# All eight transposes of a visit ahead of the two copies that empty them

## The chip, the cores and the metric

One core of a Trainium2 chip runs the whole program. The metric is the device time of one execution in microseconds; the kernel before takes 685.97 us, the median of 3 runs (685.84 to 686.15). The engines are TensorE (PE, with its weight loads shown apart as PEld), VectorE (DVE), ScalarE (ACT), GpSimd (POOL) and SyncE (SP, which here only issues DMA transfers). Every engine works through its own queue in the order in which the instructions stand there, and waits on semaphores that the others raise.

## The reference

A recurrent retention block (4 batches, 8 heads, 768 steps, head size 64) is followed by a two-layer block with a SiLU between the layers:

```python
gamma = 1.0 - 2.0 ** (-5.0 - np.arange(H, dtype=np.float32))
for t in range(S):
    state = gamma[None, :, None, None] * state + np.einsum('bhd,bhe->bhde', k[:, :, t], v[:, :, t])
    y[:, :, t] = scale * np.einsum('bhd,bhde->bhe', q[:, :, t], state)
x = y.transpose(0, 2, 1, 3).reshape(B * S, H * D)      # 3072 x 512
h = x @ w_in                                           # 512 x 2048
g = h * (1.0 / (1.0 + np.exp(-h)))
out = g @ w_out                                        # 2048 x 512
```

The two weight matrices arrive as 64-bit floats, read as pairs of 32-bit words.

## The kernel before

The 768 steps are cut into 6 chunks of 128, and a chunk of one batch is a *unit*: 24 units, chunk by chunk. A function `visit()` is called 26 times; call m works on three units at once. `stage_t(m)` transposes unit m: four 128x128 transposes of its keys (`kf`) and four of its queries (`qf`) on PE into one tile `tp` that spans two PSUM banks, keys in the first bank and queries in the second; two ACT copies bring them to SBUF as `kt` and `qt` (L289). `stage_y(m - 2)` computes that unit's output and state product on PE into a tile `y` (L305): 24 matmuls in general, fewer in the first chunk, and 16 without the state product in the last. `finish_y` splits `y` into three parts for the products that follow (ACT L364, DVE L365 and L366) and updates the state (ACT L356, DVE L358). `stage_a(m - 1)` computes the scores of unit m - 1 into a tile `sc` (PE L336), and DVE weighs them (`am`, L340). The tiles `tp`, `y` and `sc` share one PSUM pool of two buffers of two banks each, and are asked for in this order. So `sc` of a visit takes the buffer of `tp` of the same visit, and can start only after both copies have emptied it; and the next `tp` takes the buffer of `y`.

Between the visits stand the first-layer products. `product_in(c, f)` makes 12 matmuls (L413, L414, L415) into `ha` and `hb`, two buffers each, which ACT (L417, then the SiLU L419) and DVE (L418, between the two) drain; SP writes the result `g` to DRAM. Chunks 0 and 1 take 32 products, in four groups of eight written out by hand (`phases`): the first half of the weight blocks for chunk 0, then for chunk 1, then the second half for each; from chunk 2 on a visit follows every fourth product. Through the first part of the kernel, the weights are converted from 64 bits and split (`take_w`): per block of 128 rows or columns an ACT operation L172, six DVE operations from L174 to L186, and, for the first layer, two on ACT (L105, L109) and two more on DVE (L107, L110). They are waited for late: the conversions run up to eight blocks ahead of the product that needs them. After the last product the second layer runs (L533 to L535), PE alone setting its pace.

PE's order is that of the code (it is scheduled by hand). The order of ACT, DVE, POOL and SP is chosen by a list scheduler when the program is built, by its own estimate of when each instruction becomes ready; a change in the code on PE therefore moves instructions on the other engines too.

In what follows, visit m is the m-th call, counted from 0. Visits 0 to 5 stand ahead of the first product, visits 6 to 13 between the products of chunks 0 and 1, visits 14 to 23 between those of chunks 2 to 4, and visits 24 and 25 have no transposes left.

Of the kernel before, what the change touches and what calls it, by code (L numbers as in the profile page):

```python
# [12 lines left out]
FP32 = mybir.dt.float32  # L13
# [18 lines left out]
def kernel(  # L32
# [26 lines left out]
    nc = tc.nc  # L59
    B, H, S, D = q.shape  # L60
    DM, DF = moe_w_in.shape
    C = 128
    NC = S // C
    HP = H // 2
# [12 lines left out]
    def pool(name, bufs, **kw):  # L77
        return ctx.enter_context(tc.tile_pool(name=name, bufs=bufs, **kw))
# [6 lines left out]
    one = pool("one", 1)  # L85
# [30 lines left out]
    kqv = {"k": {}, "q": {}, "v": {}}  # L116
# [72 lines left out]
    evac, w_sb = [], {}  # L189
# [23 lines left out]
    ident = const.tile([128, 128], FP32, tag="ident", name="ident")  # L213
# [49 lines left out]
    xt, kt, qt, am, live = {}, {}, {}, {}, {}  # L263

    def banks(name):
        return ps_u.tile([128, 2, 512], FP32, tag="u", name=name)
# [12 lines left out]

    def stage_t(n):  # L280

        tp = banks(f"tp_{n}")
        for i, (name, src, to, bufs) in enumerate((("k", kqv["k"][n], kt, 2),
                                                   ("q", kqv["q"].pop(n), qt, 3))):
            part = tp[:, i].rearrange("p (a t) -> p a t", a=HP)
            for a in range(HP):
                nc.tensor.transpose(part[:, a, :], src[:, 2 * a : 2 * a + 2, :], ident)  # L287
            t = one.tile([128, HP, C], FP32, tag=f"{name}t", name=f"{name}t_{n}", bufs=bufs)
            evac[:] = [nc.scalar.copy(out=t, in_=part).ins]  # L289
            to[n] = t  # L290

    def stage_y(n):

# [88 lines left out]
    def visit():  # L382
        m = visits[0]
        visits[0] += 1
        if m - 2 >= len(units):
            return
        if m < len(units):
            stage_t(m)
        rest = None
        if m >= 2:  # L390
            stage_y(m - 2)
            rest = finish_y(m - 2)
        if 1 <= m <= len(units):
            stage_a(m - 1)
            scale_q(m - 1)
            scale_k(m - 1)
        if rest is not None:
            rest()
        load("k", m + 2)
        load("q", m + 2)  # L400
        load("v", m)
# [114 lines left out]
    for c in range(NC):  # L516
# [8 lines left out]
        for f in range(NF):  # L525
            n = c * NF + f
            split(n + S_AHEAD)
            t = ready.pop(n)
# [7 lines left out]
        for b in range(B):  # L536
            oa, ob = acc[b]
            o = one.tile([128, DM], FP32, tag=("kt", "qt")[b % 2], name=f"o_{c}_{b}",
                         bufs=(2, 3)[b % 2])
# [33 lines left out]
```

## Time and profile before

| | us |
|---|---|
| median of 3 runs | 685.97 |
| the profiled execution | 685.41 |
| its span, first to last instruction | 683.5 |
| PE busy in the span | 639.4 |
| DVE busy | 427.9 |
| ACT busy | 284.4 |

The profile comes from one execution. The span lies inside that execution's time, with 1.9 us around it. A row of a timeline gives the start, the duration, the engine, line and operation, the tiles as output<-input, and how many alike follow each other; in brackets stands the time that the engine idled before the row, and what ended it. A row of the waits names who waited for whom, with the total, the number of waits and the longest. A row of the windows gives the busy time of each engine in one stretch of the span and the TensorE clock that was granted there (1.00 is full). Matmuls overlap in the array, so a group's duration is from its first start to its last end.

### The profile page before, as it was taken

Reading aid. Unit: us, or ns where it says so; the run is one execution under the profiler, and the core shown is the slowest. Engines: PE = TensorE matmul, PEld = TensorE weight load, DVE = VectorE, ACT = ScalarE, POOL = GpSimd, SP = SyncE. Lnnn points to the kernel's source line nnn. Section 1 sums busy time; section 2 is a strip of 40 time slices with the busy share of each in tenths; the row PEclk is TensorE's granted clock in tenths of the full one; section 3 lists DMA queues with packets and bytes.
Section 4 is the critical chain, followed back from the end, with each engine's and each line's share of the span. In section 5 each row is a group of like instructions: output and inputs, shape, how many; then the busy total and the mean of one; then the engine's idle time right before and its main releaser. Section 6 shows DMA issues by size and latency. Waiting matters only on the chain.

```text
span 683.5 us, 11097 instructions
## 1 busy us (share of the span) xinstructions
PE 639.4 (94%) x4288; PEld 520.8 (76%) x4288; DVE 427.9 (63%) x696; ACT 284.4 (42%) x510; POOL 10.6 (2%) x44
## 2 busy tenths in 40 slices
PE   4768889899999999999999999999999999999996
PEld 3656667687877777777788888888888888888885
DVE  5878999995567675756443876546455463734641
ACT  5536545654544444544435795222222221321311
POOL 3000000000000000000000000000000000000000
PEclk9979999999999999999999999999999999999999
DMA  8865766776455666766412775334253352523401
GB/s 201 184 146 147 177 178 203 205 226 217 154 159 165 203 184 200 203 183 193 140 69 83 227 214 156 111 108 151 67 180 91 94 169 78 166 82 123 142 14 62
DMA packets 123061, 103.50 MB, mean 151 GB/s; under 512 B 80000, under 2 KB 88192, under 8 KB 123008
## 3 DMA queue, kind: packets, MB, share of 16 engines
q1 hardware_dynamic: 119552, 96.49, 48.9%
q10 hardware_dynamic: 3456, 6.29, 2.5%
q8 instruction: 34, 0.56, 0.3%
q14 instruction: 19, 0.16, 0.1%
HBM read 66.06 MB, written 36.70 MB: 150 GB/s over the span
## 4 chain that ended last, share of the span: by engine, by line
PE 79%; DVE 9%; ACT 5%; DMA 3%; issue 2%; SPq 1%; ACTq 0%; DVEq 0%
PE ha L413 11%; PE ha L414 11%; PE hb L415 11%; PE ob L535 6%; PE o L533 6%; PE o L535 6%; PE o L534 6%; PE oa L533 6%; PE oa L534 6%; PE y L305 5%; PE sc L336 2%; PE tp L287 2%; DMA wf<-in_moe_w_in_dram 2%; ACT kt L289 1%; DVE g L418 1%
## 5 line engine op out<-in xcount | busy, mean ns | idle before, releaser
L415 PE MATMUL hb<-xt,wi 128*128 128x512 f32 x384 | 151.1, 394 | 3.1 <-DVE xt L366 2.5
L413 PE MATMUL ha<-xt,wi 128*128 128x512 f32 x384 | 152.6, 397 | 0.0
L414 PE MATMUL ha<-xt,wi 128*128 128x512 f32 x384 | 150.2, 391 | 0.0
L460 DVE TENSOR_TENSOR gs<-gr,gs 128x512 fp32r<-128x512 f32 x96 | 62.1, 686 | 93.5 <-ACT gs L458 93.5
L458 ACT ACTIVATE gs<-gr 128x512 fp32r<-128x512 f32 x96 | 53.4, 621 | 139.3 <-issue 131.7
L418 DVE TENSOR_TENSOR g<-g,hb 128x512 f32<-128x512 f32 x96 | 65.8, 685 | 69.4 <-ACT g L417 67.4
L419 ACT ACTIVATE g<-g 128x512 f32<-128x512 f32 x96 | 60.7, 632 | 72.7 <-DVE g L418 71.9
L415 PEld LDWEIGHTS hb<-xt,wi 128*128 128x128 f32 x384 | 72.4, 189 | 21.0 <-DVE xt L366 2.9
L413 PEld LDWEIGHTS ha<-xt,wi 128*128 128x128 f32 x384 | 72.5, 189 | 18.0 <-issue 3.5
L414 PEld LDWEIGHTS ha<-xt,wi 128*128 128x128 f32 x384 | 72.6, 189 | 14.6
L417 ACT ACTIVATE g<-ha 128x512 f32<-128x512 f32 x96 | 56.7, 591 | 60.0 <-PE ha L414 44.0
L535 PE MATMUL ob<-wo,gs 128*128 128x512 f32 x192 | 75.3, 392 | 0.0
L533 PE MATMUL o<-wo,gs 128*128 128x512 f32 x192 | 74.8, 389 | 0.0
L533 PE MATMUL oa<-wo,gs 128*128 128x512 f32 x192 | 74.8, 389 | 0.0
L535 PE MATMUL o<-wo,gs 128*128 128x512 f32 x192 | 74.7, 389 | 0.0
L534 PE MATMUL oa<-wo,gs 128*128 128x512 f32 x192 | 74.7, 389 | 0.0
L534 PE MATMUL o<-wo,gs 128*128 128x512 f32 x192 | 74.7, 389 | 0.0
L461 DVE SCALAR_TENSOR_TENSOR gs<-gs 128x512 fp32r<-128x512 f32 x96 | 61.9, 684 | 0.0
L535 PEld LDWEIGHTS ob<-wo,gs 128*128 128x128 f32 x192 | 36.0, 188 | 8.9 <-DVE o L541 1.5
L535 PEld LDWEIGHTS o<-wo,gs 128*128 128x128 f32 x192 | 36.0, 188 | 7.6
L534 PEld LDWEIGHTS oa<-wo,gs 128*128 128x128 f32 x192 | 36.1, 188 | 7.5
L534 PEld LDWEIGHTS o<-wo,gs 128*128 128x128 f32 x192 | 36.0, 188 | 7.5
(67 smaller groups left out, 693.2 us busy)
## 6 DMA issues: line engine op xcount, KB each, us to landing
gd<-g SPq DMA_DIRECT2D x96, 256.0 KB, 2.8
gr<-gd SPq DMA_DIRECT2D x96, 256.0 KB, 2.7
wf<-in_moe_w_out_dram SPq DMA_DIRECT2D x16, 512.0 KB, 4.2
kf<-in_k_dram SPq DMA_DIRECT2D x24, 256.0 KB, 4.2
qf<-in_q_dram SPq DMA_DIRECT2D x24, 256.0 KB, 4.0
vf<-in_v_dram SPq DMA_DIRECT2D x24, 256.0 KB, 4.3
out_dram<-o ACTq DMA_DIRECT2D x24, 256.0 KB, 2.1
wf<-in_moe_w_in_dram SPq DMA_DIRECT2D x16, 256.0 KB, 3.3
```

The costliest lines, as they stand in the source:

```text
L413: nc.tensor.matmul(ha, lhsT=w[0], rhs=x[0], start=first_, stop=False)
L414: nc.tensor.matmul(ha, lhsT=w[1], rhs=x[1], start=False, stop=last)
L415: nc.tensor.matmul(hb, lhsT=w[2], rhs=x[2], start=first_, stop=last)
L417: nc.scalar.activation(out=hs, in_=ha, func=AF.Copy, scale=ONE_E)
L418: nc.vector.tensor_tensor(out=hs, in0=hs, in1=hb, op=ALU.subtract)
L419: nc.scalar.activation(out=hs, in_=hs, func=AF.Silu)
L458: nc.scalar.activation(out=t[:, 0, :], in_=g, func=AF.Copy, scale=HALF)
L460: nc.vector.tensor_tensor(out=t[:, 1, :], in0=g, in1=high, op=ALU.subtract)
L461: nc.vector.scalar_tensor_tensor(out=t[:, 2, :], in0=t[:, 1, :].bitcast(FP32), scalar=-1.0 / EPS, in1=high, op0=ALU.mult, op1=ALU.add)
L533: nc.tensor.matmul(oa, lhsT=gh, rhs=wo[f][:, 0, :], start=first_, stop=False)
L534: nc.tensor.matmul(oa, lhsT=glo, rhs=wo[f][:, 1, :], start=False, stop=last)
L535: nc.tensor.matmul(ob, lhsT=gm, rhs=wo[f][:, 2, :], start=first_, stop=last)
```

## The change

In `stage_t`, the loop that transposed the keys, copied them, transposed the queries and copied those becomes two loops: all eight transposes first, then the two copies. Tiles, buffers and computing instructions stay the same.

```diff
-        tp = banks(f"tp_{n}")
-        for i, (name, src, to, bufs) in enumerate((("k", kqv["k"][n], kt, 2),
-                                                   ("q", kqv["q"].pop(n), qt, 3))):
-            part = tp[:, i].rearrange("p (a t) -> p a t", a=HP)
+        tp = banks(f"tp_{n}").rearrange("p o (a t) -> p o a t", a=HP)
+        for i, src in enumerate((kqv["k"][n], kqv["q"].pop(n))):
             for a in range(HP):
-                nc.tensor.transpose(part[:, a, :], src[:, 2 * a : 2 * a + 2, :], ident)
-            t = one.tile([128, HP, C], FP32, tag=f"{name}t", name=f"{name}t_{n}", bufs=bufs)
-            evac[:] = [nc.scalar.copy(out=t, in_=part).ins]
-            to[n] = t
+                nc.tensor.transpose(tp[:, i, a, :], src[:, 2 * a : 2 * a + 2, :], ident)
+        for i, (name, to, bufs) in enumerate((("kt", kt, 2), ("qt", qt, 3))):
+            to[n] = one.tile([128, HP, C], FP32, tag=name, name=f"{name}_{n}", bufs=bufs)
+            evac[:] = [nc.scalar.copy(out=to[n], in_=tp[:, i]).ins]
```

The lines behind `stage_t` move up by two: L287 becomes L285, both copies L288, L336 becomes L334 and so on.

On PE, at visit 14 (`tp` is the tile of the transposes, `y` and `sc` those of the two products behind them; a wait is named after the engine or DMA queue that raises the semaphore), the rows before are:

```order
L287 MATMUL tp_2185<-ident,kf_1596 128x128 [waits DMAHW3_49,PE_49]
L287 MATMUL tp_2185<-ident,qf_1598 128x128 [waits DMAHW4_49,Activation_49]
L305 MATMUL y_2198<-vf_1600,kf_1246 64x64 [waits DMAHW1_49,PE_49]
L305 MATMUL y_2198<-am_1717,vf_1600 64x128 x8
L305 MATMUL y_2198<-qt_1544,state_242 64x128 x8
L336 MATMUL sc_2227<-qt_1669,kt_1663 64x128 [waits Activation_49]
```

and those of the change:

```order
L285 MATMUL tp_2185<-ident,kf_1596 128x128 [waits DMAHW4_49,PE_49]
L285 MATMUL tp_2185<-ident,qf_1598 128x128 [waits DMAHW7_49]
L303 MATMUL y_2198<-vf_1600,kf_1246 64x64 [waits DMAHW5_49,PE_49]
L303 MATMUL y_2198<-am_1717,vf_1600 64x128 x8
L303 MATMUL y_2198<-qt_1544,state_242 64x128 x8
L334 MATMUL sc_2227<-qt_1669,kt_1667 64x128 [waits PE_49,Activation_49]
```

PE's order is the same; the transposes of the queries no longer wait for ACT, and `sc` still does.

On ACT, at visit 10 (`g` is drained from the products, `ca`, `wi` and `wil` belong to the weight conversion, `ys` takes `y` away), the rows before are:

```order
L172 ACTIVATE ca_1166<-wf_1014 128x512 [waits DMAHW1_49,DMAHW7_49,DMAHW0_49,DVE_49]
L417 ACTIVATE g_5_1158<-ha_5_1144 128x512 [waits DMAHW4_49,PE_49,Activation_49]
L289 COPY kt_1188<-tp_1183 128x512 [waits PE_49]
L105 ACTIVATE wi_1137<-cs_1128 128x512 [waits DVE_49]
L289 COPY qt_1194<-tp_1183 128x512 [waits PE_49]
L419 ACTIVATE g_5_1158<-g_5_1158 128x512 [waits DVE_49]
```

and those of the change:

```order
L415 ACTIVATE g_5_1158<-ha_5_1144 128x512 [waits DMAHW4_49,PE_49,Activation_49]
L172 ACTIVATE ca_1166<-wf_1014 128x512 [waits DMAHW1_49,DMAHW2_49,DMAHW0_49,DVE_49]
L288 COPY kt_1192<-tp_1183 128x512 [waits PE_49]
L288 COPY qt_1194<-tp_1183 128x512
L417 ACTIVATE g_5_1158<-g_5_1158 128x512 [waits DVE_49]
```

The two copies stand side by side, and the second has no wait of its own: the first already waits for all eight transposes. `ca` has moved between the drain of `ha` and the copies. In the visits of the later chunks (visit 14 among them) the SiLU L419 stays between the two copies, as before.

On DVE, ahead of the weighing of the scores at visit 13 (`am`; `cs`, `cp`, `ca`, `wil` and `wi` belong to the weight conversion), the rows before are:

```order
L107 SCALAR_TENSOR_TENSOR wil_1527<-cs_1517,wi_1526 128x512
L110 SCALAR_TENSOR_TENSOR wi_1526<-wi_1526,wil_1527 128x512
L174 TENSOR_SCALAR cs_1642<-wf_1475 128x512
L179 SCALAR_TENSOR_TENSOR cs_1642<-ca_1641,cs_1642 128x512
L358 TENSOR_TENSOR state_245<-state_245,y_1671 128x256
L181 TENSOR_SCALAR cp_1643<-cs_1642 128x512
L176 TENSOR_SCALAR ca_1824<-ca_1824 128x512
L183 SCALAR_TENSOR_TENSOR cp_1643<-wf_1475,cp_1643 128x512
L340 TENSOR_TENSOR am_1717<-sc_1700,decay 128x1024
```

and those of the change:

```order
L181 TENSOR_SCALAR cp_1518<-cs_1517 128x512
L356 TENSOR_TENSOR state_245<-state_245,y_1671 128x256
L183 SCALAR_TENSOR_TENSOR cp_1518<-wf_1367,cp_1518 128x512
L176 TENSOR_SCALAR ca_1641<-ca_1641 128x512
L186 TENSOR_TENSOR cs_1517<-cs_1517,cp_1518 128x512
L338 TENSOR_TENSOR am_1717<-sc_1700,decay 128x1024
L107 SCALAR_TENSOR_TENSOR wil_1527<-cs_1517,wi_1526 128x512
L278 TENSOR_TENSOR qt_1544<-qt_1544,gq 128x512
L110 SCALAR_TENSOR_TENSOR wi_1526<-wi_1526,wil_1527 128x512
```

`am` has moved from place 199 of DVE's queue to place 192: seven operations of the weight conversion that stood ahead of it now stand behind it. From the visit before that on to the products behind it, the drains and weighings stand two to four microseconds of DVE work nearer the front than before (by the durations that DVE's rows have in the trace); by the drain of the twenty-fourth product both orders have done the same work.

## The prediction

> **What bounds the kernel now.** I read the busy times first, then the same by stages.
>
> ```profile
> PE 639.4 (94%) x4288; PEld 520.8 (76%) x4288; DVE 427.9 (63%) x696; ACT 284.4 (42%) x510; POOL 10.6 (2%) x44
> 0.00:47.00 47.00, 28.09 (x338) 21.45 (x338) 33.77 (x53) 23.06 (x54) 5.16 (x40) 0.93 0.88 191
> 47.00:137.00 90.00, 77.37 (x858) 62.24 (x862) 82.24 (x141) 49.28 (x86) 2.71 (x2) 0.94 0.65 175
> 137.00:155.00 18.00, 17.76 (x95) 14.16 (x88) 16.66 (x31) 8.53 (x16) 0.00 (x0) 1.00 0.78 236
> 155.00:193.00 38.00, 38.00 (x168) 31.01 (x169) 19.60 (x32) 19.95 (x35) 0.00 (x0) 1.00 0.51 169
> 193.00:351.00 158.00, 150.86 (x1328) 123.16 (x1327) 101.88 (x165) 72.03 (x122) 2.72 (x2) 1.00 0.60 177
> 351.00:683.00 332.00, 327.28 (x1515) 268.74 (x1513) 173.73 (x277) 111.60 (x200) 0.00 (x0) 1.00 0.38 121
> ```
>
> A stage's row is its length, then PE, PEld, DVE, ACT and POOL busy, the granted clock, the DMA share and GB/s. The 94% is an average over stages with different limits. From 193 to 351 us (visits 14 to 23) PE is idle for 158.00 - 150.86 = 7.1 us and DVE is busy for only 64%: PE sets the time. From 47 to 137 us (visits 6 to 13) DVE is busy for 82.24 of 90 us and PE for 77.37: there DVE is the fuller engine. Up to 47 us neither is full. Behind 351 us no transpose is left, and I expect nothing to change.
>
> Next, who waited for whom: up to 155 us (first three rows), in its part from 47 to 137 us (the fourth), and from 155 to 352 us (the last).
>
> ```profile
> PE tp L287 <- ACT kt L289: 15.7, 14, 2.8
> PE hb L415 <- DVE xt L366: 2.5, 1, 2.5
> PE sc L336 <- ACT qt L289: 2.1, 3, 1.1
> PE tp L287 <- ACT kt L289: 10.3, 8, 2.8
> PE tp L287 <- ACT kt L289: 6.8, 10, 0.7
> ```
>
> In all 24 visits the transposes of the queries wait for the copy of the keys: 22.5 us in sum, 6.8 of it in the ten late visits. That wait the change takes away. The question is how much comes back as a wait of `sc`, which needs both copies, and how much the full DVE of the early stage swallows.
>
> **The late visits (14 to 23): 6.6 us.** Visit 14, in order of time:
>
> ```profile
> 192.86 0.60 PE L287 MATMUL tp<-ident,kf 128*128 128x128 f32 x4
> 192.88 0.60 ACT L417 ACTIVATE g<-ha 128x512 f32<-128x512 f32 x1 [0.73 <-PE ha L414]
> 193.50 0.59 ACT L289 COPY kt<-tp 128x512 f32<-128x512 f32 x1
> 193.51 0.69 DVE L418 TENSOR_TENSOR g<-g,hb 128x512 f32<-128x512 f32 x1 [2.03 <-ACT g L417]
> 194.13 0.66 PE L287 MATMUL tp<-ident,qf 128*128 128x128 f32 x4 [0.68 <-ACT kt L289]
> 194.23 0.63 ACT L419 ACTIVATE g<-g 128x512 f32<-128x512 f32 x1 [0.15 <-DVE g L418]
> 194.72 0.69 PE L305 MATMUL y<-vf,kf 128*64 128x64 f32 x16
> 194.83 0.59 ACT L289 COPY qt<-tp 128x512 f32<-128x512 f32 x1
> 195.24 1.05 PE L305 MATMUL y<-am,vf 128*64 128x128 f32 x16
> 196.70 1.05 PE L336 MATMUL sc<-qt,kt 64*64 64x128 f32 x32
> ```
>
> Four transposes take 0.60 us, of which the last one's own 0.27 overlaps what follows, so they are about 0.11 apart and the fifth can start some 0.45 us behind the first, at 193.31 instead of 194.13. `y` starts 0.59 us behind that (194.72 - 194.13), at 193.90, and PE is ready for `sc` 1.98 us later (196.70 - 194.72), at 195.88: 0.82 us earlier.
>
> ACT is late next. The first copy now waits for all eight transposes, which end at 193.31 + 0.66 = 193.97; with the 0.04 us that lie between the transposes' end and the copy in these rows it runs from 194.01 to 194.60. The SiLU behind it (its input is ready when L418 ends, 194.20) runs to 195.25 and the second copy to 195.86. So `sc` may start at about 195.9, just when PE is there. I take 0.8 us a visit; the bounds are 0.5 (another 0.3 us of handing over on ACT) and 0.9.
>
> Visits 22 and 23 have a shorter `y`. Visit 23:
>
> ```profile
> 336.04 0.60 PE L287 MATMUL tp<-ident,kf 128*128 128x128 f32 x4
> 337.31 0.66 PE L287 MATMUL tp<-ident,qf 128*128 128x128 f32 x4 [0.68 <-ACT kt L289]
> 339.41 1.05 PE L336 MATMUL sc<-qt,kt 64*64 64x128 f32 x32
> ```
>
> Here `sc` stood 339.41 - 336.04 = 3.37 us behind the first transpose. ACT's chain (copy, SiLU, copy) takes 195.9 - 192.86 = 3.04 us as at visit 14, so it ends last, and 0.3 us is gained. The sum is 8 x 0.8 + 2 x 0.3 = 7.0; I take 6.6, nearer to the lower bound since ACT has nothing to spare, with ends at 4.5 and 7.8.
>
> **The first 47 us: 1.8 us.** The first product that needs a whole chunk starts at 47.22 us, behind DVE's last split L366 (the 2.5 us above). DVE comes to that split through this row:
>
> ```profile
> 42.91 0.69 DVE L365 TENSOR_TENSOR xt<-y,xt 128x512 fp32r<-128x512 f32 x1 [1.79 <-ACT xt L364]
> ```
>
> DVE stood idle for 1.79 us, for a `y` that stands behind two of the waits removed. An earlier `y` gains at most this idle time, then DVE's other work is in the way. The bounds are 0 and 5.4 (all waits of the first six visits, 15.7 - 10.3). I take 1.8.
>
> **Visits 6 to 13: 5.7 us.** PE's waits look large here, and the longest is at visit 10:
>
> ```profile
> 87.91 0.60 PE L287 MATMUL tp<-ident,kf 128*128 128x128 f32 x4
> 89.67 0.67 ACT L172 ACTIVATE ca<-wf 128x512 f32<-128x512 f32 x1 [0.43 <-DVE cs L179]
> 90.23 0.58 ACT L417 ACTIVATE g<-ha 128x512 f32<-128x512 f32 x1
> 90.71 0.58 ACT L289 COPY kt<-tp 128x512 f32<-128x512 f32 x1
> 91.35 0.87 PE L287 MATMUL tp<-ident,qf 128*128 128x128 f32 x4 [2.84 <-ACT kt L289]
> 93.06 1.92 PE L305 MATMUL y<-am,vf 128*64 128x128 f32 x16
> ```
>
> ACT came late to the copy because `ca` ahead of it waited for DVE. The change lets PE go through the transposes and `y` meanwhile, so this wait shrinks to what is left at `sc`. Besides, behind the wait of 2.84 us the same 16 matmuls of `y` take 1.92 us, against 1.05 at visit 14 (the row at 195.24): the granted clock is lower there (0.94 in the stage), and an unbroken PE would keep it.
>
> But DVE decides what of this stays. It has 90 - 82.24 = 7.8 us of idle time in the stage, and PE waits for its drains and weighings, whatever PE gained. Two things let PE run ahead of it. First, order: at visit 13 seven conversion operations move behind `am`. Their cost is from these two rows, between which eight operations of DVE start:
>
> ```profile
> 135.41 0.68 DVE L107 SCALAR_TENSOR_TENSOR wil<-cs,wi 128x512 f32<-128x512 f32 x1
> 139.58 1.22 DVE L340 TENSOR_TENSOR am<-sc,decay 128x1024 f32<-128x1024 f32 x1
> ```
>
> (139.58 - 135.41) / 8 = 0.52 us each, so 3.6 us. Second, idle time: DVE idles partly because its inputs from PE come late; I take a quarter of the 7.8 us, 2.1 with rounding up. Together 5.7 us. The bounds are 0 (DVE's idle time stays, and the work put off is in the way later) and 3.6 + 7.8 = 11.4.
>
> Is the work put off paid for later? These rows speak of it:
>
> ```profile
> 154.13 0.68 DVE L418 TENSOR_TENSOR g<-g,hb 128x512 f32<-128x512 f32 x1
> 154.86 0.50 PE L415 MATMUL hb<-xt,wi 128*128 128x512 f32 x1 [0.24 <-DVE g L418]
> 161.42 0.69 DVE L186 TENSOR_TENSOR cw<-cs,cp 128x512 f32<-128x512 f32 x1 [1.12 <-DMA wod<-cw]
> ```
>
> At 154 us PE runs into DVE's backlog, for 0.24 us; at 161 DVE already idles, and the backlog is gone. A product takes 12 matmuls of 38.00 / 168 = 0.226 us (the row from 155 to 193 us, where PE never idles), 2.7 us, and with two buffers PE can be a product ahead of the drains. So most of 5.7 us can stay; more than about 8 (5.7 and most of a product) would meet the drains around 160 us.
>
> One rule of the skill speaks against this part. Perfetto Trace Analysis in the Trainium skill (section Identifying Performance Opportunities) says to judge by the engine with the highest occupancy in each regime, and to optimize that one first. Here that is DVE with 82.24 of 90 us, by the row above; by the rule alone a change that only takes waits from PE would be worth nothing in these visits. It is the first rival below.
>
> **Sum.** 1.8 + 5.7 + 6.6 = 14.1 us. Against the profiled execution, 685.41 - 14.1 = 671.3; the median of the runs is 0.56 us above that execution, so 671.9 us.
>
> **Rivals.**
> *DVE holds the first 155 us.* All early waits turn into waits for DVE, and only the late visits count: 685.97 - 6.6 = 679.4. For it: DVE's 91% from 47 to 137 us. Against it: DVE itself idled for PE and ACT, and the order puts work behind. Chance 0.10.
> *All named waits go.* Early, the 15.7 us of `tp`, the 2.1 of `sc`, and the slower clock behind the long wait of visit 10 (1.92 - 1.05 = 0.9) vanish, with the 6.6 us late: 685.97 - 25.3 = 660.7. Against it speaks DVE's idle time: of 25.3 - 6.6 = 18.7 us, 13.3 (without the 5.4 of the first six visits) is more than DVE can give up between 47 and 137 us. Chance 0.08.
> *The wait only moves.* ACT hands over later than I reckon, and `sc` waits as long as the transposes did: 686.0. In the late visits this takes a second copy that ends 0.8 us later than worked out; the rows give no cause. Chance 0.03.
> *Slower: the copies stand behind a conversion that waits.* At visit 10 `ca` now stands ahead of both copies, and it needs a weight load and DVE. Before, such waits for the load were 3.5 us in two visits:
>
> ```profile
> ACT ca L172 <- DMA wf<-in_moe_w_in_dram: 3.5, 2, 2.6
> wf<-in_moe_w_in_dram SPq DMA_DIRECT2D x16, 256.0 KB, 3.3
> ```
>
> A load takes 3.3 us to land. If its issue slips behind the loads of keys, which now wait for other transposes, each such visit loses up to 3.3 us at `sc`. It decides from 14.1 / 3.3 = 4.3 visits on; with all of the eight, 685.97 - 14.1 + 26.4 = 698.3, with five 688.4. Chance 0.04.
>
> **How the numbers follow.** The forecast, 671.9, has 0.75. Its own ends are the bounds of its terms: all three at their upper ends give 5.4 + 11.4 + 7.8 = 24.6, but the drains around 160 us let no more than about 8 of the middle term through, and the first is held by DVE's idle time: 1.8 + 8 + 7.8 = 17.6, so 668.4, to which I add 1.4 for what the first may exceed it by; at the other end stands the first rival, 679.4, with 0.10, which the range takes in. I give 667.0 to 679.5, which leaves out the second, third and fourth rivals, 0.15. Faster by more than 0.2% (1.4 us, about what a measurement of this kernel can tell from no change) has 0.93, the rest 0.03 and 0.04.
>
> **What would show it.** The row of `tp` waiting for `kt` is gone. In the late visits the first and fifth transposes stand 0.45 us apart, `sc` about 3.0 us behind the first transpose (3.84 before), and waits of `sc` for `qt` are below 0.2 us except at visits 22 and 23 (about 0.3 to 0.5). Visit 14 starts about 7.5 us earlier than 192.86, visit 23 about 14 earlier than 336.04. Between visits 6 and 13 `sc` waits for `qt` in most visits, DVE is busy for over 93%, and the two long waits do not come back whole. I am wrong if visit 14 starts near 191 or later (DVE holds it), or below 182 (DVE was never the limit), or if `sc` waits 0.5 us or more in every late visit.

## The result, and the profile after

| | before | after |
|---|---|---|
| median, us | 685.9 (4 runs beside it) | 669.66 (4 runs, 669.1 to 670.51) |
| ratio, with its 95% interval | | 0.9766 [0.9749, 0.9783] |
| the profiled execution, us | 685.41 | 669.9 |
| its span, us | 683.5 | 667.8 |

The change is faster by 2.3%. The page's busy times, and windows near the stages of before (length, then PE, PEld, DVE, ACT and POOL busy, granted clock, DMA share, GB/s):

```profile
PE 631.8 (95%) x4288; PEld 515.8 (77%) x4288; DVE 423.9 (63%) x696; ACT 282.0 (42%) x510; POOL 10.5 (2%) x44
0.00:44.00 44.00, 22.99 (x338) 18.01 (x338) 32.94 (x53) 22.54 (x54) 5.88 (x40) 0.96 0.90 191
44.00:128.00 84.00, 75.44 (x871) 61.21 (x871) 77.00 (x135) 47.83 (x84) 2.45 (x2) 0.96 0.72 188
128.00:147.00 19.00, 19.00 (x83) 15.39 (x84) 18.13 (x33) 10.96 (x19) 0.00 (x0) 1.00 0.74 224
147.00:185.00 38.00, 37.42 (x163) 29.43 (x162) 21.29 (x35) 19.07 (x34) 0.00 (x0) 1.00 0.56 185
185.00:336.00 151.00, 150.32 (x1329) 123.25 (x1328) 100.82 (x165) 69.60 (x123) 2.18 (x2) 1.00 0.62 185
336.00:667.00 331.00, 326.62 (x1512) 268.49 (x1512) 173.76 (x277) 112.02 (x200) 0.00 (x0) 1.00 0.38 121
```

Stage by stage, in whole microseconds, the lengths went 47 to 44, 90 to 84, 18 to 19, 38 to 38, 158 to 151 and 332 to 331. The late visits (185 to 336) are now full on PE: 0.7 us of idle time where 7.1 stood. The middle stage lost 6 us, and DVE's idle time in it hardly changed (84.00 - 77.00 = 7.0 us, against 7.8): DVE simply does 82.24 - 77.00 = 5.2 us less of its work in there. Some of that work shows again in the next two stages, where DVE is busy for 39.4 us against 36.3.

These windows are cut by hand and do not hold the same work (871 matmuls against 858 in the second). Cut at the starts of visits 6, 13 and 14 they do, but for one matmul at an edge; three rows of the kernel before, then three of the change:

```profile
0.00:51.20 51.20, 32.07 (x348) 24.57 (x349) 36.78 (x58) 23.09 (x55) 5.16 (x40) 0.90 0.81 177
51.20:132.23 81.03, 69.70 (x773) 56.02 (x772) 74.53 (x127) 45.12 (x79) 2.71 (x2) 0.96 0.68 182
132.23:192.86 60.63, 59.31 (x329) 48.14 (x328) 40.96 (x70) 32.49 (x57) 0.00 (x0) 1.00 0.60 191
0.00:48.21 48.21, 26.97 (x349) 21.03 (x350) 36.31 (x59) 23.35 (x56) 5.88 (x40) 0.93 0.90 188
48.21:123.63 75.42, 67.19 (x774) 54.69 (x773) 69.84 (x122) 43.13 (x75) 2.45 (x2) 0.98 0.71 188
123.63:184.63 61.00, 60.31 (x329) 47.96 (x328) 43.21 (x75) 33.56 (x58) 0.00 (x0) 1.00 0.63 199
```

From visit 6 to visit 13 the stage is 5.6 us shorter; DVE is busy in it for 4.7 us less and idle for 0.9 us less. PE's side is less plain than its waits suggest. Visit 14 starts 8.2 us earlier, but PE's idle time ahead of it shrinks by only 31.8 - 30.2 = 1.6 us; the other 6.6 us are busy time, for the same matmuls at a higher granted clock (0.93 against 0.90, then 0.98 against 0.96). At visit 10 the transposes of the queries and `y` ran at 0.58 behind the long wait and run at 1.00 now (before, then the change, whose row takes in two matmuls at its edge):

```profile
91.35:95.45 4.10, 4.10 (x52) 3.44 (x56) 3.93 (x7) 2.27 (x4) 0.00 (x0) 0.58 0.61 165
81.44:84.13 2.69, 2.69 (x54) 2.11 (x52) 2.66 (x6) 0.48 (x1) 0.00 (x0) 1.00 0.15 57
```

Whether the clock makes the early gain is taken up with the first experiment.

PE's longer waits up to 155 us (who waited for whom, total, number, longest), and in the last row its waits from 185 to 325 us, all that the view lists:

```profile
PE tp L285 <- DMA kf<-in_k_dram: 10.5, 3, 6.7
PE sc L334 <- ACT qt L288: 8.1, 5, 2.3
PE tp L285 <- ACT state L354: 4.5, 3, 2.3
PE hb L413 <- DVE xt L364: 3.4, 1, 3.4
PE y L303 <- DVE am L338: 1.5, 3, 0.6
PE hb L413 <- DVE g L416: 0.4, 2, 0.2
```

The row of `tp` waiting for `kt` is gone. In the early part 8.1 us of waits stand at `sc`, where 2.1 stood before, all between 44 and 128 us. The two long waits came back for the most part: 2.26 of 2.84 us at visit 10, 2.11 of 2.47 at visit 12. In the late visits the view lists no wait of `sc` at all. Visit 14 and visit 10, in order of time:

```profile
184.63 0.60 PE L285 MATMUL tp<-ident,kf 128*128 128x128 f32 x4
185.07 0.60 PE L285 MATMUL tp<-ident,qf 128*128 128x128 f32 x4
185.71 0.59 ACT L288 COPY kt<-tp 128x512 f32<-128x512 f32 x1 [0.45 <-PE tp L285]
186.19 0.63 ACT L417 ACTIVATE g<-g 128x512 f32<-128x512 f32 x1
186.72 0.58 ACT L288 COPY qt<-tp 128x512 f32<-128x512 f32 x1
187.58 1.05 PE L334 MATMUL sc<-qt,kt 64*64 64x128 f32 x32
```

```profile
81.01 0.60 PE L285 MATMUL tp<-ident,kf 128*128 128x128 f32 x4
82.49 1.04 PE L303 MATMUL y<-am,vf 128*64 128x128 f32 x16
84.71 0.66 ACT L172 ACTIVATE ca<-wf 128x512 f32<-128x512 f32 x1
85.28 0.57 ACT L288 COPY kt<-tp 128x512 f32<-128x512 f32 x1
85.75 0.59 ACT L288 COPY qt<-tp 128x512 f32<-128x512 f32 x1
86.39 0.88 PE L334 MATMUL sc<-qt,kt 64*64 64x128 f32 x23 [2.26 <-ACT qt L288]
```

At visit 14 the second copy ends at 187.30, 0.28 us before `sc`: ACT hands over in time. At visit 10 it doesn't. PE now goes on through the transposes and `y` (1.04 us for the 16 matmuls that took 1.92 behind the old wait, at the lower clock) and then waits 2.26 us at `sc`, where the copies come late behind `ca`. Even so `sc` stands 86.39 - 81.01 = 5.38 us behind the first transpose; before, the trace had it at 95.45 - 87.91 = 7.54.

### The profile page after: what moved, and what is told of

The parts are those of the page before. It is cut to its first block, busy times and chain, and to the rows that moved or that the text cites. A ratio compares the mean times of both kernels' runs of the same rounds, so it can differ in the third digit from the quotient of the medians.

```text
span 667.8 us, 11107 instructions
## 1 busy us (share of the span) xinstructions
PE 631.8 (95%) x4288; PEld 515.8 (77%) x4288; DVE 423.9 (63%) x696; ACT 282.0 (42%) x510; POOL 10.5 (2%) x44
## 4 chain that ended last, share of the span: by engine, by line
PE 77%; DVE 9%; DMA 5%; ACT 5%; issue 2%; SPq 1%; ACTq 0%; DVEq 0%
PE ha L411 11%; PE hb L413 11%; PE ha L412 11%; PE ob L533 7%; PE o L531 6%; PE o L533 6%; PE o L532 6%; PE oa L531 6%; PE oa L532 6%; DMA wf<-in_moe_w_in_dram 4%; PE y L303 2%; PE sc L334 2%; PE tp L285 1%; DVE g L416 1%; DVE am L338 1%
## 5 line engine op out<-in xcount | busy, mean ns | idle before, releaser
L416 DVE TENSOR_TENSOR g<-g,hb 128x512 f32<-128x512 f32 x96 | 65.7, 684 | 60.4 <-ACT g L415 59.9
```

Of the source, the lines that this page charges most:

```text
L416: nc.vector.tensor_tensor(out=hs, in0=hs, in1=hb, op=ALU.subtract)
```

## The experiments

A useful measure beside the time is the *lead*: how much earlier the first transpose of a visit starts than in the kernel before. It shows where in the program a gain arises and where it is lost. The starts come from the timelines of the profiled executions:

| kernel | visit 6 | visit 13 | visit 14 | visit 23 | span | lead at 6 | at 13 | at 14 | at 23 | at the end |
|---|---|---|---|---|---|---|---|---|---|---|
| before | 51.20 | 132.23 | 192.86 | 336.04 | 683.5 | | | | | |
| the change | 48.21 | 123.63 | 184.63 | 321.05 | 667.8 | 2.99 | 8.60 | 8.23 | 14.99 | 15.7 |
| the change, a second trace | 48.47 | 123.91 | 185.25 | 322.43 | 669.2 | 2.73 | 8.32 | 7.61 | 13.61 | 14.3 |
| late visits alone | 51.32 | 131.86 | 192.92 | 329.06 | 675.7 | -0.12 | 0.37 | -0.06 | 6.98 | 7.8 |
| early visits alone | 48.75 | 123.90 | 185.93 | 329.08 | 676.4 | 2.45 | 8.33 | 6.93 | 6.96 | 7.1 |
| first six alone | 49.59 | 129.14 | 190.28 | 333.42 | 680.7 | 1.61 | 3.09 | 2.58 | 2.62 | 2.8 |
| visits 6 to 13 alone | 50.81 | 125.66 | 188.07 | 331.23 | 678.7 | 0.39 | 6.57 | 4.79 | 4.81 | 4.8 |
| before, no clamp | 46.01 | 125.32 | 186.20 | 328.90 | 676.3 | 5.19 | 6.91 | 6.66 | 7.14 | 7.2 |
| change, no clamp | 43.84 | 117.22 | 179.93 | 315.91 | 662.8 | 7.36 | 15.01 | 12.93 | 20.13 | 20.7 |
| change, conversions later | 47.53 | 121.63 | 184.60 | 320.71 | 667.7 | 3.67 | 10.60 | 8.26 | 15.33 | 15.8 |
| before, conversions later | 49.37 | 129.13 | 192.42 | 335.58 | 682.9 | 1.83 | 3.10 | 0.44 | 0.46 | 0.6 |
| change, SiLU behind the copies | 48.17 | 120.72 | 183.56 | 318.62 | 665.1 | 3.03 | 11.51 | 9.30 | 17.42 | 18.4 |
| change, clamp on GpSimd | 52.56 | 126.84 | 190.94 | 340.58 | 687.3 | -1.36 | 5.39 | 1.92 | -4.54 | -3.8 |
| the same, SiLU behind the copies | 51.44 | 123.19 | 187.62 | 336.57 | 683.1 | -0.24 | 9.04 | 5.24 | -0.53 | 0.4 |

One execution stands behind each row. The two traces of the change differ by 0.6 us at visit 14 and by 1.4 at visit 23, so a difference of leads below about 1 us says little.

### Which visits carry the gain

Four kernels hold both forms of `stage_t` and choose by the visit. The edit, with the condition of each:

```diff
+    def stage_t(n):
+        (stage_t_together if n >= 14 else stage_t_apart)(n)   # late
+        (stage_t_together if n < 14 else stage_t_apart)(n)    # early
+        (stage_t_together if n < 6 else stage_t_apart)(n)     # first six
+        (stage_t_together if 6 <= n < 14 else stage_t_apart)(n)  # 6 to 13
```

Late visits alone:

> Transposes together only from visit 14 on, apart before that. If PE sets the time of the late visits, their part of the gain comes alone and whole: the trace of the change shows 7.5 us there (lead at the end of the span 15.7 less the lead at visit 14, 8.2), so about 685.9 - 7.5 = 678.4. If the early lead made room for it (ACT and DVE had less left over when the late visits began), less: 681 or more.

Measured 677.8 us, ratio 0.9875 [0.9823, 0.9926].

Early visits alone:

> Transposes together only in visits 0 to 13. By the sum of parts 685.9 - 8.2 = 677.7. If DVE's backlog was what the early lead came from and is paid back when the late visits keep their waits, the lead at visit 14 (8.2 us) would shrink behind it: 680 or more.

Measured 678.01 us, ratio 0.987 [0.9837, 0.9903].

The first six alone:

> Transposes together only in visits 0 to 5. The trace of the change has a lead of 3.0 us where the first product meets the last split. If leads add up: 682.9. If DVE, full in visits 6 to 13, sets the time there whatever came before, but from an earlier start, also near 682.9; if it swallows the lead because the same conversions stand in the way later, 685 to 686.

Measured 682.26 us, ratio 0.9933 [0.9908, 0.9957].

Visits 6 to 13 alone:

> Transposes together only in visits 6 to 13. By the sum of parts 685.9 - 5.2 = 680.7 (lead 8.2 at visit 14 less 3.0). If the middle would have reached the same point without the early lead (DVE's order decides, not the start): 677.7 to 678. If DVE holds it: 685 or more.

Measured 681.58 us, ratio 0.9919 [0.9894, 0.9944].

The kernel before stood at 686.11 beside them, so the gains are 8.3, 8.1, 3.9 and 4.5 us. Late and early add up to 16.4, the whole change (685.9 - 669.66 = 16.2); the first six and visits 6 to 13 add up to 8.4, the early change. The parts are nearly independent of each other, as far as the intervals let one say (that of the late visits alone runs from 5.1 to 12.1 us). In the table the early gains are kept to the end, but for 0.5 to 1.8 us that is lost between visits 13 and 14. Visits 6 to 13 gain where their edit stands; of the gain of the first six, 1.6 us is there at visit 6 and the rest arises behind it.

Is the early gain one of the clock, since PE's busy time fell so much? Two traces speak against the clock as its main cause. In the kernel with the late visits alone, whose early visits have the old form, PE is busy for 30.60 us up to visit 6 (32.07 before) and for 68.66 up to visit 13 (69.70), and visit 14 starts no earlier. In the second trace of the change PE is busy for 28.23 us up to visit 6 instead of 26.97, and visit 6 starts only 0.26 us later: in both, less busy time is more idle time. No run holds the clock fixed, so its share between visits 6 and 13 stays open.

### Does DVE's work set the time of the early stage?

The conversion has a clamp on DVE (L176). It is left out here, once in the kernel before and once in the change; the outputs then lack that clamp.

```diff
-        nc.vector.tensor_scalar(out=a.bitcast(FP32), in0=a.bitcast(FP32),
-                                scalar1=bits(1024 << 20), scalar2=bits((1279 << 20) - 1),
-                                op0=ALU.max, op1=ALU.min)
```

Before without the clamp:

> The kernel before without the clamp of the weight conversion (DVE L176, left out; 0.42 us of DVE for each of 32 blocks, 9 of them between 47 and 137 us). If DVE sets the time of visits 6 to 13, these 9 x 0.4 = 3.6 us and a part of those before 47 us come off: 681 to 683. If PE's own waits for the copies set it, the time stays within 1 us of 686.

Measured 678.21 us against 685.49, ratio 0.9872 [0.9839, 0.9905]. PE's waits up to 155 us, in that kernel:

```profile
PE tp L284 <- ACT kt L286: 16.0, 14, 3.4
```

The change without the clamp:

> The change without the same clamp. If DVE is still what holds visits 6 to 13 (it is busy for 77.0 of the 84 us there), about 3.6 us come off again: 665 to 667. If PE has become the limit, 669 to 670.

Measured 665.09 us, ratio 0.969 [0.9659, 0.9722], 4.6 us below the change.

The clamps up to 155 us in the kernel before are this group (of the costliest lines, up to 155 us):

```profile
L176 DVE TENSOR_SCALAR ca<-ca 128x512 f32<-128x512 f32 x19 | 8.0, 423 | 4.2 <-ACT ca L172 4.1
```

Without them the kernel before is 7.3 us faster, while the wait that the change removes stays whole (16.0 us against 15.7). That is more than was expected, and it does not arise where it was looked for: at visit 6 this kernel is already 5.2 us ahead, of the 6.7 at visit 14, and the change without the clamp is 4.4 us ahead of the change (48.21 - 43.84), of 4.7. Only five of the 20 clamps up to visit 14 stand ahead of visit 6, and ten between visits 6 and 13. But the list scheduler moved other work as well, as DVE's busy time in these two stretches of the kernel without the clamp shows:

```profile
0.00:46.01 46.01, 28.18 (x349) 21.42 (x350) 32.28 (x49) 22.62 (x55) 5.26 (x40) 0.93 0.91 189
46.01:125.32 79.31, 68.99 (x773) 55.88 (x772) 72.33 (x121) 45.02 (x78) 1.91 (x2) 0.96 0.72 186
```

Ahead of visit 6 DVE is busy for 36.78 - 32.28 = 4.5 us less, where five clamps make 2.1; from visit 6 to 13 for 74.53 - 72.33 = 2.2 us less, where ten make 4.2. Over both it does 6.7 us less, and visit 13 comes 6.9 us earlier. That fits DVE's work setting the time of the early part as a whole; and the length of the wait of `tp` for `kt` does not say what its removal is worth. The pair does not show that DVE holds visits 6 to 13, as the expectations had it; the number of the second came true (665 to 667), but not where it was to arise. Nor does it separate three things: the clamp as work, the clamp as a link in the chain from `ca` to `cs`, and the order that the list scheduler chose.

### Is it the order on DVE?

The conversions of a place are written behind the visit instead of ahead of it, in the change and in the kernel before:

```diff
-            if i in takes:
-                take_w()
             if i in at:
                 visit()
+            if i in takes:
+                take_w()
```

In the change `am` of visit 13 then stands at place 184 of DVE's queue (192 in the change, 199 before):

> The change with each weight conversion of visits 6 to 13 written behind its visit instead of ahead of it, so that the list scheduler puts it further back on DVE and ACT. If the lead in these visits comes from conversions moving behind the weighings and drains, more of that gives more: 1 to 4 us less, 666 to 668.5. If it comes from the wait on PE alone, no change: 669 to 670.5. If the backlog is then in the way of the products behind visit 13, more than 670.5.

Measured 669.54 us, ratio 0.976 [0.9729, 0.9791]: no gain over the change. The expectation fell, and the table shows how: visit 13 comes 2.0 us earlier than in the change, and visit 14 at the same time. Between the two, PE has two waits of 1.5 us in sum, where the change has one of 0.4:

```profile
125.91 1.10 PE L334 MATMUL sc<-qt,kt 64*64 64x128 f32 x32 [1.16 <-ACT qt L288]
136.40 0.50 PE L413 MATMUL hb<-xt,wi 128*128 128x512 f32 x1 [0.31 <-DVE g L416]
```

In the kernel before, the same move puts `am` at place 191, about where the change has it, and keeps the waits of `tp`:

> The kernel before (copies apart, every wait of the transposes kept) with each weight conversion of visits 6 to 13 written behind its visit. Its queue for DVE then has the weighing of visit 13 at place 191, against 199 before and 192 in the change. If the order alone, without the wait, gives what visits 6 to 13 gained, this kernel has a lead of 4 to 5 us at visit 14 and takes 681 to 682. If taking the wait from PE is needed as well, the transposes wait as before for a copy that is late, the lead stays under 2 us, and it takes 684 to 686.

Measured 684.24 us against 685.81, ratio 0.9983 [0.9965, 1.0001]. The wait is there as before (first row, up to 155 us); of the 3.10 us that visit 13 leads, 0.44 is left at visit 14, and PE shows a new wait for a SiLU between 128 and 193 us (second row):

```profile
PE tp L287 <- ACT kt L289: 15.1, 14, 2.5
PE ha L413 <- ACT g L417: 1.3, 1, 1.3
```

So the order alone is worth next to nothing, and removing the waits is needed too (whether the waits alone would do, in the old order, no run shows); and work put off beyond what the waits free is given back before visit 14. The rest of the give-back is no wait. Between the starts of visits 13 and 14 PE is busy for longer over the same 329 matmuls, at a granted clock of 1.00: 61.23 us against 60.31 in the change, and 60.51 against 59.31 in the kernel before. What makes them longer stays open.

### Can ACT hand over sooner?

The SiLU that stands ahead of a visit is queued behind both copies:

```diff
+        def last(after=None):
+            with tc.issue_after(after) if after else ExitStack():
+                nc.scalar.activation(out=hs, in_=hs, func=AF.Silu)
+        silu.append(last)
+        if not hold:
+            silu.pop()()
...
+        while silu:                     # in visit(), behind stage_t
+            silu.pop()(evac[0])
```

> The change with the SiLU of the product ahead of a visit queued behind both copies on ACT, in visits 6 to 23. Late: the scores wait for the second copy by 0.2 to 0.3 us in five visits of ten in the trace of the change, so about 1.2 us come off. Early: PE's waits of the scores for the second copy are 8.1 us in visits 6, 8, 10, 11 and 12; if they set the time, up to 5 more come off (663 to 664), if DVE does, none (668 to 669).

Measured 668.12 us (667.02 to 669.84), ratio 0.9736 [0.9704, 0.9769]. The interval overlaps that of the change, so 1.5 us is not settled by the times. The traces speak for it, though: from visit 14 to 23 the lead grows by 8.1 us (6.8 and 6.0 in the two traces of the change), since `sc` stands 2.48 us behind the first transpose at visit 23 (321.10 - 318.62) instead of 2.71. Early, the wait of `sc` for `qt` falls

```profile
PE sc L334 <- ACT qt L288: 4.7, 3, 2.2
```

from 8.1 to 4.7 us, and visit 14 gains only 1.1 us from that. Its median is the lowest here of a kernel that computes the whole reference.

### The clamp on GpSimd

If DVE's work is what counts, another engine could take the clamp. Beside it ran the change once more, and the same edit with the SiLU behind the copies.

```diff
-        nc.vector.tensor_scalar(out=a.bitcast(FP32), in0=a.bitcast(FP32),
+        nc.gpsimd.tensor_scalar(out=a.bitcast(FP32), in0=a.bitcast(FP32),
```

The change again:

> The change itself, beside the two kernels below on the same chip: 669 to 670.5 by its runs so far.

Measured 670.46 us, ratio 0.9781 [0.9747, 0.9816].

The clamp on GpSimd:

> The change with the clamp of the weight conversion moved from DVE to GpSimd, which is idle for 98% of the span. If DVE's load is what is left in the early stage, it gains what leaving the clamp out gained, 4 to 5 us: 665 to 666. If the longer way through GpSimd (its 128x512 products take 1.04 us against 0.42 on DVE) delays the conversions or slows DVE, 667 to 670 or more.

Measured 688.88 us, ratio 1.0047 [1.003, 1.0064].

With the SiLU behind the copies:

> The same with the SiLU behind both copies besides. If the two gains add up (4.5 and 1.5 us): 663 to 664.5. If the SiLU's gain comes from the early visits alone and DVE no longer holds them, more: 661 to 663.

Measured 685.35 us, ratio 1.0001 [0.9983, 1.002].

The gain that was hoped for failed by more than 20 us in both. The first kernel's groups up to 155 us, then two rows of its timeline in a late visit, then a wait from 186 to 345 us:

```profile
L176 POOL TENSOR_SCALAR ca<-ca 128x512 f32<-128x512 f32 x19 | 39.1, 2057 | 101.4 <-ACT ca L172 101.4
L179 DVE SCALAR_TENSOR_TENSOR cs<-ca,cs 128x512 uint32<-128x512 uint32 x19 | 13.1, 689 | 10.2 <-POOL ca L176 9.3
```

```profile
194.26 1.92 POOL L176 TENSOR_SCALAR ca<-ca 128x512 f32<-128x512 f32 x1 [35.92 <-ACT ca L172]
196.21 0.69 DVE L179 SCALAR_TENSOR_TENSOR cs<-ca,cs 128x512 uint32<-128x512 uint32 x1 [3.34 <-POOL ca L176]
```

```profile
PE hb L413 <- DVE g L416: 10.3, 8, 1.7
```

One clamp takes 2057 ns there, against 423 on DVE. DVE is rid of 8 us of work, and stands idle for 9.3 us in the early part because the next operation of its queue waits for the clamp. In the late visits the drains L416 are queued behind that stalled operation, and PE waits 10.3 us for them: visit 23 is 4.54 us *behind* the kernel before, where visit 14 was still 1.92 ahead. The price had been taken from the row of another operation (1.04 us for a product of two tiles), not of this one; and an operation moved off the full engine helps only if its result comes back before that engine reaches the next operation in its queue.

## Why the prediction was right, point by point

Forecast 671.9 us, measured 669.66. By the leads, the terms against what was measured:

| term | forecast | measured | from |
|---|---|---|---|
| the first 47 us | 1.8 | 3.0 | 47.22 - 44.23, the first `hb` behind DVE's split |
| visits 6 to 13 | 5.7 | 5.2 | 8.23 - 2.99, the lead at visit 14 less that at visit 6 |
| from visit 14 on | 6.6 | 7.5 | 15.7 - 8.23, the lead at the end less that at visit 14 |

**The late visits.** The mechanism held, seen row by row: first to fifth transpose 0.44 us, `sc` 2.95 us behind the first transpose at visit 14, visit 23 at 321.05. The size is less sure than 7.5 looks: the second trace of the change gives 14.3 - 7.61 = 6.7, and the late-visits kernel, which shows the term by itself, 7.8 + 0.06 = 7.9. What the rows do show is that ACT's chain was mis-sized. The prediction let each of copy, SiLU and copy begin where the one before ended; the rows of visit 14 start 0.48 and 0.53 us apart, though they last 0.59 and 0.63, so the second copy ends 187.30 - 184.63 = 2.67 us behind the first transpose, not 3.00. (The prediction's own rows of visit 10 have it: 90.23 + 0.58 = 90.81, and the next starts at 90.71.) The Trainium skill (ScalarE: Activation LUTs, section What ACT_TABLE_LOAD costs) states that back-to-back ACTIVATEs overlap by about 93 ns. The rows here agree, with 0.11 and 0.10 us, for copies too. Hence little of a wait was left. At visit 23 `sc` still stands on the copy, by less than the view of waits lists: it starts 2.71 us behind the first transpose, and 2.48 where the SiLU is out of the way. It gained 3.37 - 2.71 = 0.66 us where 0.3 was reckoned.

**The first 47 us.** The bound chosen, DVE's 1.79 us of idle time ahead of its split, was too tight. The kernel with the first six visits alone has visit 13 3.09 us ahead and ends 2.8 ahead. One row shows that the stage still ends in that wait,

```profile
44.23 0.50 PE L413 MATMUL hb<-xt,wi 128*128 128x512 f32 x1 [3.37 <-DVE xt L364]
```

3 us earlier and with PE waiting longer. Part of what was freed became waits for key loads: PE's `tp` waits for `kf` for 10.5 us (7.1 before). The step that failed is that DVE's other work would be in the way. These rows, of the kernel before and of the change, show it moved:

```profile
40.69 0.43 DVE L176 TENSOR_SCALAR ca<-ca 128x512 f32<-128x512 f32 x1 [0.42 <-ACT ca L172]
39.62 0.69 DVE L363 TENSOR_TENSOR xt<-y,xt 128x512 fp32r<-128x512 f32 x1
```

Before, the split stood behind this clamp, which itself waited for 0.42 us; in the change it stands ahead of the clamp and finds DVE without idle time, behind an operation (L186) that starts 39.58 - 39.01 = 0.57 us earlier. With the 1.79 us this makes about 2.8 of the 3.0.

**Visits 6 to 13.** The sum came out and its parts did not, which is luck. Order was to give 3.6 and DVE's idle time 2.1; by the rows cut at the visits DVE's idle time gave 0.9 and work put off 4.7, 0.4 of which is lost up to visit 14. That DVE is the fuller engine and yet lets PE gain was right: visits 6 to 13 alone gave 4.5 us. The rule from the Trainium skill that the prediction weighed (Perfetto Trace Analysis, section Identifying Performance Opportunities), to judge by the engine with the highest occupancy, would have given nothing there by the prediction's reading. (The same section would have TensorE judged by its arithmetic rate or its weight loads; by the loads, PEld's 62.24 of 90 us, DVE is still the fuller.) The measurement goes against that reading (ratio 0.9919 [0.9894, 0.9944]). The pair without the clamp fits DVE's work as a limit of the early part as a whole, with most of the lead ahead of visit 6; it does not place that limit in these visits. PE could run ahead, it seems, because some of DVE's queue was work that nobody yet waited for: the 4.7 us speak for it, but no run takes the waits away and keeps the old order, so it is argued, and so is the clock's share. The cap of about 8 us was argued from one short wait at 154 us; the kernels that move the conversions later show a cap at work, since 10.60 us of lead at visit 13 shrinks to 8.26 at visit 14.

**The signs.** One missed: DVE was to be busy for over 93% between visits 6 and 13, and was for 77.00 / 84 = 92%; the stage shrank as much as DVE's work in it. `sc` was to wait for `qt` in most of these visits, and did in five of eight.

**The rivals.** DVE holds the first 155 us: fell with the early kernel (8.1 us). All named waits go: fell, 8.1 us stand at `sc`. The wait only moves: so it did early in part (at visits 10 and 12 for the most part), late hardly. Copies behind a conversion that waits: the mechanism is there at visit 10 (2.26 us), cheaper than the wait of 2.84 us that it replaced.

## What to carry to other kernels

When one engine fills a tile in two halves and another empties it, finish all writes before the first read is queued: here the reader of the first half held up the writer of the second half, though nothing in the data asked for it. Price what comes next by starts in the trace (when the next row of the same engine starts), not by adding durations. Read from the starts where a gain arises before naming the stage that an engine holds: most of the lead without the clamps stood at visit 6 already, ahead of where DVE was fullest. And where another engine is nearly full, ask which of its queued work is not yet needed; work moved back further than the waits free is given back later, and moving it to a slower engine can stall the queue that it was meant to empty.

## What the hardware showed unexpectedly

ACT's operations of 128x512 start 0.47 to 0.53 us apart when their inputs are ready, though each row lasts 0.57 to 0.63 us (85.28 and 85.75 at visit 10; 185.71, 186.19 and 186.72 at visit 14). The two-operation clamp of 128x512 takes 2057 ns on GpSimd and 423 ns on DVE, nearly five times as long; spans on GpSimd are rough in this profile, but DVE's next operation starts 0.03 us behind the end of that row (196.21 against 194.26 + 1.92). At visit 10 the same transposes and `y` ran at a granted clock of 0.58 behind a wait of 2.84 us and at 1.00 without it.
